# Attention with softmax split between ScalarE and VectorE: score units evacuated in pairs from two neighbouring PSUM banks

## The chip, the cores and the metric

The kernel runs on one core of a Trainium2 chip. The metric is device time in microseconds (us), the median of several executions. Engine names: TensorE (PE in the profile; PEld is its weight load), VectorE (DVE), ScalarE (ACT), GpSimd (POOL) and SyncE (SP), which issues DMA transfers. PSUM is the accumulator memory that TensorE writes: 8 banks, each holding 128x512 values of fp32 in this kernel.

## The reference

One transformer block with adaptive layer norm, for 2048 tokens of width 640, 32 heads of 20 columns, in bf16. The vector c gives six modulation rows (shift, scale and gate of each half).

```python
h = _layernorm(x) * (1 + ca) + sa
qkv = (h @ wqkv).reshape(B, S, 3, H, Dh)           # H = 32, Dh = 20
scores = einsum('bhqd,bhkd->bhqk', q, k) * Dh ** (-0.5)
o = einsum('bhqk,bhkd->bhqd', softmax(scores), v)
x = x + ga * (o @ wo)
h = _layernorm(x) * (1 + cb) + sb
x = x + gb * (((h @ w_gate) * (h @ w_up)) @ w_down)   # F = 1536
```

The scores are 32 x 2048 x 2048 numbers, and each goes through an exponential.

## The kernel before, in words

**Chunks, items, units.** The queries are cut into five chunks (`CHUNKS`: three of 512 and two of 256). A chunk has eight items; an item is four heads, one on each 32-row strip of TensorE. The scores of an item are made in units: one head's 128x512 block of transposed scores, which fills one PSUM bank (in a chunk of 256 queries a unit holds two key blocks). A score visit of TensorE (line 1403) writes several units; units on different row strips run side by side.

**Two ways to the exponential.** Most units go to ScalarE. Two or three of them form a group, which lies in neighbouring banks and is read by one ACTIVATE (line 1439, `fexp`) of 128x1024 or 128x1536 into the buffers PP. Even groups use set A of banks, odd ones set B; group g of `glist` is scored as soon as ScalarE has read the group before it in the same set. From group 580 (`HEADG`) on, even groups have three units.

The other units go to VectorE. They come in quads of four units, one per row strip; `QUADS` gives the number of quads of each item. A unit of a quad is scored as a passenger of a score visit (`d_attach`), into a bank of the shared pool G. VectorE evacuates it with one TENSOR_SCALAR of 128x512 (line 1463, `fp1`, called P1) into a quarter of a DB buffer as int16: add a bias, clamp at zero. This number's bits, read as bf16, approximate the exponential. When the quad is whole, two bit operations of 128x2048 (lines 1495 and 1503) and one multiplication (line 1500) make two correction terms in DSS, both of which TensorE multiplies with V (line 1957), beside the exponentials of ScalarE.

**What else uses PSUM.** Bank 7 collects the output of the current item. Pool G (banks 5, 6 and 2) also serves every round of the other stages: projections (lines 1062, 1126), V, output projection and feed-forward (lines 862 and 866), transposes and warm-up rounds. GX and GC serve the head of the program. Set A has banks 0, 1 (and 2 from group 580 on, when it leaves G), set B banks 3 and 4.

**What sets the order.** A planner written into the kernel (`Sched`) makes the order of every engine when the program is built: it steps through an assumed time with assumed durations, and emits fixed instruction streams with semaphore waits. `pick_pe` chooses TensorE's next work: a score visit if its banks are free, else value products, else rounds of other stages. `d_attach` adds up to two quad units to a visit, if in the planner's time a bank of G is free and the unit is due (`due`, from `D_LEAD`). Rounds of the other stages have a gate, a group number before which they may not start (`GATE_F`, `LATE_A`, `LATE_L`); `steal` gives ScalarE an evacuation when it would idle. The constants at the top steer these choices.

**The suffix.** After each chunk come its output projection, second layer norm and feed-forward. That of one chunk is spread between the visits of the next chunk; that of the last chunk stands behind the last exponential: output projection (line 862), residual sum (1682), statistics (1696), normalisation (1703), transposes (1715), evacuation with scale and shift into h2Tc (1731 and 1733), gate and up rounds (862), product hprodc (1784), down projection, residual sum (1838), store. The matmuls that remain of the fourth chunk's down projection (line 866, wd and hprodt) stand in between. With `T_SPLIT` the h2Tc evacuations of the last chunk are made per 128 tokens.

Of the kernel before, what the change touches and what calls it, by code (L numbers as in the profile page):

```python
# [12 lines left out]
SEM = 60.0  # L13
# [12 lines left out]
DMA_SLOW = 0.0015  # L26
DMA_LAT = 1700.0
STEAL_END = 66197.894
STEAL_GAP = 184.697
HAM_W = 3413.3  # L30
HAM_MIN = 2550.0

# [288 lines left out]
def emit_program(nc, sched, nsem_dma=56):  # L321
# [83 lines left out]
    with nc.Block() as block:  # L405
# [20 lines left out]
        def _(e):  # L426
# [4 lines left out]
CHUNKS = ((0, 512), (512, 512), (1024, 512), (1536, 256), (1792, 256))  # L431
QUADS = ((0, 4, 3, 3, 4, 3, 4, 3),
         (3, 4, 3, 4, 3, 3, 4, 4),
         (3, 3, 4, 4, 3, 4, 4, 4),
         (1, 2, 1, 2, 1, 1, 1, 2),
         (1, 1, 1, 1, 0, 1, 1, 1))
D_LEAD = 0.383
NB0, NSS = 2, 3
HEADG = 580
OP_EARLY = 1  # L440
EV_OP = 0.5
T_SPLIT = 1
GU_OUTER = 4
TAIL_PRE = 1
LN2T = 0.6
# [2 lines left out]
X_LAST = 2  # L448
X_TAIL = 0
XBACK = 1  # L450
HOLD = 110
PVTOL = 253
XDPRIO = 2.163
TPRIO = 0.75
TAHEAD = 1
GU_ONE = 1
# [3 lines left out]
NPS = 4  # L460
TS_4X, TT_2X = 600.0, 1145.0
WM_GATE = 9
WM_NEED = 1.814
K_DIRECT = (0, 1, 2, 3)
Q_DIRECT = 2
K_LEAD = 0.705
K_ALL = (0,)
KD_LEAD = 0.216
DMA_WINDOW = 900000
D_LATE = 16  # L470
D_RES = 58
PVMIN, PVMAX, PVCAP = 4, 14, 13
PV0 = 0
V_PARTS = [[0, 4], [4, 8]]
V_L1 = 0.2
# [7 lines left out]
PREEMPT = 0.0  # L483
PRE_M = 0.3
PV0N = 1
GATE_F = (0.925, 0.688, 1.105, 0.744, 1.0)
FILL_MIN = 4156.882
FILL_HARD = 0.0
FILL_T0, FILL_TH, FILL_MINH = 2300.0, 17000.0, 7500.0
FILL_MODE = 'P'  # L490
# [2 lines left out]
LN_POOL = ()  # L493
LN_ACT = [1, 3, 5, 7]
XFIRST = 0
LN2P = 2.447
NALT = 1
OPFIRST = 0
HT_L = 0.105
V_L = 0.225  # L500
LATE_A = 4.5
LATE_L = 2.493
LATEQ = (3,)
LATEQ_A = 2
LATEQ_F = 0.581
QUAD_GAIN = 0.597233983857778
NTERM = 2
XHALF = 1
X_LATE = -0.231
X_HALF = 0.0  # L510


# [8 lines left out]
def build_kernel(nc, A_x, A_wqkv, A_wo, B_x, B_w_gate, B_w_up, B_w_down, c, w_mod, out):  # L521
# [53 lines left out]
    def bank(b):  # L575
        return ps[:, b, :]
# [112 lines left out]
            stx.append(C.alloc("stx", [128, 2, KD, 128], BF16))  # L689
        nsq, nsx = nsx, len(stx)  # L690

    G = Slots([5, 6, 2] if HEADG else [5, 6], "G")
    GX = Slots([3, 4] if HEADG else [2, 3, 4], "GX")
    hx = (1, 3) if HEADG else (1, 3, 4)
    GC = Slots([0, 1], "GC")
    BPV = 7
# [577 lines left out]
    while ap < NA:  # L1274
        even = len(glist) % 2 == 0
        us = ubuf[ap:ap + (3 if even and len(glist) >= HEADG else 2)]
        apos.append(ap)
        ap += len(us)
        glist.append((us, 0 if even else 3))
    NG = len(glist)  # L1280
    sc.ng = NG
    gstart = []
# [109 lines left out]
    def unit_score_deps(u):  # L1392
        d = list(qt_ready[(u.j, u.ci)])
        for kt in u.kts:
            hv = kt_half.get((u.j, kt // 4))
            d += kt_ready[(u.j, kt // 4)] if hv is None else [hv[kt % 4 // 2]]
        d = list(dict.fromkeys(d))
        return d
# [58 lines left out]
    for qi, (it, us) in enumerate(dquads):  # L1457
        st_ = d_state[qi]
        for x, u in enumerate(us):
            cell = {}  # L1460

            def fp1(e, st_=st_, x=x, cell=cell):
                return e.tensor_scalar(DB0[:, st_["slot"], x * 512:(x + 1) * 512], bank(cell["b"]), EBIAS, 0.0,  # L1463
                                       op0=ALU.add, op1=ALU.max)
            tp = Task("dve", ps_cost(512), fp1, [], prio=0.8, name=f"P1.{qi}.{x}")
            tp.on_start = lambda task, cell=cell: G.done(cell["b"], task)
            u.task = (tp, cell)
            sc.left += 1
            st_["p1"][x] = tp
# [644 lines left out]
    def d_attach(ts, t, pos, rows, limit, relax):  # L2114
        n = 0
        while n < limit:
            if not dst["left"]:
                if dst["next"] >= len(dlist) or due[dst["next"]] > pos:
                    break
                dst["left"] = list(dlist[dst["next"]:dst["next"] + 4])  # L2120
                dst["fresh"] = True
            if due[dst["next"]] > pos:
                break
            pick = None
            for u in dst["left"]:
                if (u.s not in rows or relax) and all(d.done is not None and d.done + SEM <= t for d in unit_score_deps(u)):
                    pick = u
                    break
            if pick is None:
                break  # L2130
            ga = G.avail()
            if ga is None or ga[0] > t:
                break
            st_ = d_state[pick.quad[0]]
            if dst["fresh"]:
                ba = sB0.avail()
                if ba is None or ba[0] > t:
                    break
                st_["slot"], rel = sB0.take(ba[1], NTERM)
                st_["brel"] = rel  # L2140
                dst["fresh"] = False
            b, rel = G.take(ga[1], 1)
            tp, cell = pick.task
            cell["b"] = b
            ts.deps = ts.deps + unit_score_deps(pick) + rel
            ts.emits = ts.emits + unit_score_emits(pick, lambda b=b: bank(b))
            tp.deps = [ts] + st_["brel"]
            sc.left -= 1
            sc.add(tp)
            rows[pick.s] = rows.get(pick.s, 0) + 1  # L2150
            dst["left"].remove(pick)
            dst["next"] += 1
            n += 1
        return n

    def pick_pe(t):
# [44 lines left out]
        elif not tail_added[0]:  # L2201
            tail_added[0] = True
            la = [a for a in act_tasks[-2:]]
            if all(a.done is not None for a in la):
                for b in range(5):
                    if b != 2 or not HEADG or back[0]:
                        G.add(b, la)
            else:
                tail_added[0] = False
# [143 lines left out]
```

## Time and profile before

| | us |
|---|---|
| median of 3 executions | 817.66 |
| lowest, highest | 817.46, 822.7 |
| the profiled execution | 816.77 |
| its span, first to last instruction | 815.0 |
| first exponential of line 1439 starts | 16.3 |
| last exponential ends | 782.4 |
| transpose of the last item of each chunk (line 1587) | 218.6, 402.4, 585.1, 686.1, 783.1 |

Read from the profiled execution: "busy" is the time in which an engine had an instruction of the kind in work; "x" is how many; the number behind the comma is the mean length of one in ns; what stands behind the bar is idle time just ahead of it, and what ended it. Records of neighbouring instructions on one engine overlap, so the mean length is more than the time from one start to the next. A row of the stretches has the window, its length, the busy time, the count, the clock that TensorE was granted (1.00 is full), the share of DMA and GB/s; an instruction that crosses an edge counts in both windows. A row of the waits has who waited, for whom, the sum in us, how often, and the longest. A row of the timeline has start and length in us, with equal neighbours merged.

### The profile page before, as it was taken

How to read it: one execution, taken by the hardware profiler on the slowest of the kernel's cores; microseconds unless marked ns; L12 is line 12 of the kernel's file. 1: busy time of each engine (PE TensorE's matmuls, PEld its weight loads, DVE VectorE, ACT ScalarE, POOL GpSimd, SP SyncE). 2: the span in 40 equal slices, each digit the busy share in tenths (PEclk: the TensorE clock that was granted, in tenths of full speed). 3: DMA queues.
4: the chain of work that ended last, by engine and by line, in shares of the span. 5: the costliest groups of instructions: out<-in, count | busy, mean ns of one | idle time of the engine just before them, and what ended most of it. 6: DMA issues, size and time to landing. Idle time of an engine off the chain costs nothing.

```text
span 815.0 us, 29082 instructions
## 1 busy us (share of the span) xinstructions
PE 787.8 (97%) x12581; PEld 306.3 (38%) x12581; DVE 722.7 (89%) x1272; ACT 775.9 (95%) x821; POOL 73.3 (9%) x105
## 2 busy tenths in 40 slices
PE   9999999999999999999999999999989999999998
PEld 4433333322232332233333223333243344554557
DVE  7989999999989999999999999999998877676663
ACT  6889999999999999999999999999999999999952
POOL 3300000000011000000001000000021000000000
PEclk9999999999999999999999999999999999999999
DMA  9724311113500225100400222002100236116610
GB/s 294 222 84 103 77 39 38 49 49 116 126 19 25 51 66 160 39 5 28 95 6 12 49 53 55 6 20 61 47 8 14 55 86 130 44 31 137 133 37 17
DMA packets 116446, 54.73 MB, mean 67 GB/s; under 512 B 83915, under 2 KB 116319, under 8 KB 116319
## 3 DMA queue, kind: packets, MB, share of 16 engines
q1 hardware_dynamic: 115391, 51.72, 24.8%
q8 instruction: 100, 1.64, 0.9%
q10 hardware_dynamic: 928, 1.15, 0.4%
q14 instruction: 27, 0.22, 0.1%
HBM read 41.85 MB, written 8.41 MB: 62 GB/s over the span
## 4 chain that ended last, share of the span: by engine, by line
ACT 44%; PE 37%; issue 9%; DVE 9%; DMA 1%; ACTq 0%; DVEq 0%
ACT PP L1439 44%; PE ps_all L1403 11%; PE ps_all L866 10%; PE ps_all L1957 7%; DVE DB L1463 3%; PE ps_all L862 3%; PE ps_all L1126 3%; PE ps_all L1062 2%; DVE DSS L1500 1%; DMA wm<-in_w_mod_dram 1%; DVE DSS L1495 1%; DVE DSS L1503 1%; PE ps_all L1023 1%; PE ps_all L887 0%; DVE st L1696 0%
## 5 line engine op out<-in xcount | busy, mean ns | idle before, releaser
L1439 ACT ACTIVATE PP<-ps_all 128x1024 bf16<-128x1024 f32 (+1 forms) x777 | 756.9, 1202 | 5.4 <-PE ps_all L1403 3.9
L1403 PE MATMUL ps_all<-QT,KT 32*128 32x512 bf16 (+1 forms) x2560 | 309.0, 340 | 17.4 <-ACT PP L1439 13.5
L1463 DVE TENSOR_SCALAR DB<-ps_all 128x512 int16<-128x512 f32 x396 | 263.1, 682 | 35.4 <-PE ps_all L1403 34.2
L1403 PEld LDWEIGHTS ps_all<-QT,KT 32*128 32x128 bf16 x2560 | 81.5, 91 | 262.3 <-ACT PP L1439 232.4
L1957 PE MATMUL ps_all<-PP,Vf 128*32 128x512 bf16 (+2 forms) x2092 | 164.3, 342 | 0.1
L1500 DVE TENSOR_TENSOR DSS<-DB,DSS 128x2048 bf16<-128x2048 bf16 x99 | 122.0, 1232 | 0.0
L866 PE MATMUL ps_all<-h2T,stg 128*32 128x512 bf16 (+1 forms) x1808 | 116.7, 338 | 1.6 <-DVE DB L1463 1.1
L1592 POOL TENSOR_TENSOR OTn<-OT,invT 128x512 bf16<-128x512 f32 (+1 forms) x39 | 43.1, 1104 | 604.8 <-DVE invT L1590 604.8
L1957 PEld LDWEIGHTS ps_all<-PP,Vf 128*32 128x32 bf16 (+1 forms) x2092 | 47.2, 94 | 85.2 <-issue 78.5
L1957 PE MATMUL ps_all<-DSS,Vf 128*32 128x512 bf16 (+3 forms) x936 | 77.4, 350 | 0.2
L1495 DVE TENSOR_SCALAR DSS<-DB 128x2048 int16<-128x2048 int16 x99 | 68.2, 689 | 0.8
L1503 DVE TENSOR_SCALAR DSS<-DB 128x2048 int16<-128x2048 int16 x99 | 68.1, 688 | 0.9 <-PE ps_all L1957 0.9
L866 PE MATMUL ps_all<-wd,hprod 128*32 128x320 bf16 (+1 forms) x1364 | 57.9, 280 | 0.1
L866 PEld LDWEIGHTS ps_all<-h2T,stg 128*32 128x32 bf16 x1808 | 40.3, 95 | 36.9 <-issue 17.1
L866 PEld LDWEIGHTS ps_all<-wd,hprod 128*32 128x32 bf16 x1364 | 30.7, 96 | 18.4 <-issue 10.4
L866 PE MATMUL ps_all<-wV,hT 128*32 128x320 bf16 (+1 forms) x704 | 31.6, 289 | 0.1
L1957 PEld LDWEIGHTS ps_all<-DSS,Vf 128*32 128x32 bf16 (+1 forms) x936 | 23.4, 95 | 21.9 <-issue 9.1
L1126 PE MATMUL ps_all<-hT,wq 128*32 128x512 bf16 x375 | 31.1, 382 | 0.2
L1815 DVE TENSOR_TENSOR hprod<-ps_all,gsb 128x512 bf16<-128x512 f32 x36 | 24.6, 684 | 6.0 <-PE ps_all L866 6.0
L866 PE MATMUL ps_all<-wo,Ocp 128*32 128x320 bf16 (+1 forms) x620 | 28.8, 288 | 0.4 <-DVE DB L1463 0.2
L1587 DVE STREAM_TRANSPOSE OT<-ps_all 128x512 f32<-128x512 f32 (+1 forms) x40 | 24.2, 604 | 4.3 <-PE ps_all L1957 4.2
L2277 PE MATMUL ps_all<-ident 128*32 128x512 bf16 x308 | 27.3, 383 | 0.3 <-DVE DB L1463 0.2
(122 smaller groups left out, 516.8 us busy)
## 6 DMA issues: line engine op xcount, KB each, us to landing
stg<-in_B_w_gate_dram SPq DMA_DIRECT2D x50, 160.0 KB
stg<-in_B_w_up_dram SPq DMA_DIRECT2D x50, 160.0 KB
QT<-q_rows SPq DMA_DIRECT2D x22, 128.0 KB
KT<-k_rows SPq DMA_DIRECT2D x84, 32.0 KB
wm<-in_w_mod_dram SPq DMA_DIRECT2D x3, 800.0 KB
x<-in_A_x_dram SPq DMA_DIRECT2D x7, 320.0 KB
xck<-in_A_x_dram SPq DMA_DIRECT2D x3, 640.0 KB
wd<-in_B_w_down_dram SPq DMA_DIRECT2D x1, 1920.0 KB
```

What stands on the lines that cost most here:

```text
L866: return lambda e, b: e.matmul(ps[32 * x:32 * x + 32, b, c0 + o:c0 + o + w], lhs()[:, 32 * x:32 * x + 32], rhs() if w == n else rhs()[:, o ...
L1126: f = [lambda e, b_, k=k, x=x: e.matmul(ps[x:x + min(32, w - x), b_, :], wx[:, k, r0 + x:r0 + min(x + 32, w)], hT[tc][:, k, :], tile_posit ...
L1403: ems.append(lambda e, i=i, kt=kt: e.matmul(dstf()[:, i * u.n:(i + 1) * u.n], KT[32 * u.s:32 * u.s + 32, u.j, kt * 128:(kt + 1) * 128], QT ...
L1439: return e.activation(PPs[g % 2][:, cellp["p"], 0:nu * 512], ps[:, b0:b0 + nu, :].rearrange("p b c -> p (b c)"), AFT.Exp, scale=ESCALE)
L1463: return e.tensor_scalar(DB0[:, st_["slot"], x * 512:(x + 1) * 512], bank(cell["b"]), EBIAS, 0.0, op0=ALU.add, op1=ALU.max)
L1495: return e.tensor_scalar(DSS[:, st_["ss"][0], :], DB0[:, st_["slot"], :], 0x7F, 0x3F00, op0=ALU.bitwise_and, op1=ALU.bitwise_or)
L1500: return e.tensor_tensor(d, DB0[:, st_["slot"], :].bitcast(BF16), d, ALU.mult)
L1503: return e.tensor_scalar(DSS[:, st_["ss"][1], :], DB0[:, st_["slot"], :], 0x7F80, 2, op0=ALU.bitwise_and, op1=ALU.bitwise_or)
L1592: f3 = lambda e: e.tensor_tensor(OTn[:, 0:n].rearrange("p (b c) -> p b c", c=32), OT[:, 0:n].rearrange("p (b c) -> p b c", c=32), invT[:, ...
L1815: f = lambda e: e.tensor_tensor(hprod[:, fc, 0:n], ps[:, r.b["b"], 0:n], gsb[:, gs, 0:n], ALU.mult)
L1957: ems.append(lambda e, i=i, kt=kt, stt=stt, stp=stp: e.matmul(ps[32 * s:32 * s + mc, BPV, 0:u.n], Vf[:, (kt * H + 4 * u.j + s) * VW:(kt * ...
L2277: task.emits = [lambda e, x=x: e.matmul(ps[32 * x:32 * x + 32, b_, :].rearrange("p (a b) -> p a b", a=4), ident[:, 32 * x:32 * x + 32], id ...
```

## The change

When a unit of a quad is attached to a score visit, a second unit of the same quad is now looked for (its inputs there, its row strip not used in the visit, due as well). If in the planner's time two neighbouring shared banks are free, (3, 4) or else (2, 3), both are scored in that visit, into these banks, and one TENSOR_SCALAR of 128x1024 evacuates both; the output goes to two quarters of DB, which need not lie side by side. Otherwise a unit goes alone, as before. The planner counts 1120 ns for a pair.

So that the shared banks are neighbours, the bank map changes: G is now banks 4, 3 and 2, and set B (the odd groups) and GX are banks 5 and 6. Some thirty constants of the planner differ, among them the quads per item (chunk 2 has one fewer, the last chunk two more), the leads and gates, the limit of value products per turn (`PVCAP`), and `T_SPLIT`, which is off.

```diff
-STEAL_GAP = 184.697
+STEAL_GAP = 115.475
...
-         (3, 3, 4, 4, 3, 4, 4, 4),
+         (3, 3, 4, 4, 3, 4, 4, 3),
          (1, 2, 1, 2, 1, 1, 1, 2),
-         (1, 1, 1, 1, 0, 1, 1, 1))
-D_LEAD = 0.383
+         (2, 1, 1, 1, 0, 2, 1, 1))
+D_LEAD = 0.34
...
-T_SPLIT = 1
+T_SPLIT = 0
...
-K_LEAD = 0.705
+K_LEAD = 0.693
...
-D_RES = 58
-PVMIN, PVMAX, PVCAP = 4, 14, 13
+D_RES = 114
+PVMIN, PVMAX, PVCAP = 4, 14, 10
...
-GATE_F = (0.925, 0.688, 1.105, 0.744, 1.0)
+P1_PAIR = 1
+P1_PCOST = 1120.0
+GATE_F = (0.91, 0.621, 0.409, 0.425, 1.0)
...
-LATE_A = 4.5
-LATE_L = 2.493
+LATE_A = 3.033
+LATE_L = 3.352
...
-    G = Slots([5, 6, 2] if HEADG else [5, 6], "G")
-    GX = Slots([3, 4] if HEADG else [2, 3, 4], "GX")
+    G = Slots([4, 3, 2], "G")
+    GX = Slots([5, 6], "GX")
...
-        glist.append((us, 0 if even else 3))
+        glist.append((us, 0 if even else 5))
...
             def fp1(e, st_=st_, x=x, cell=cell):
+                if len(cell["bs"]) == 2:
+                    (ba, bb), (xa, xb) = cell["bs"], cell["xs"]
+                    return e.tensor_scalar(
+                        DB0[:, st_["slot"], :].rearrange("p (x c) -> p x c", c=512)[:, xa:xb + 1:xb - xa, :],
+                        ps[:, ba:bb + 1:bb - ba, :], EBIAS, 0.0, op0=ALU.add, op1=ALU.max)
...
-            b, rel = G.take(ga[1], 1)
+            mate = None
+            if P1_PAIR and limit - n >= 2:
+                for u in dst["left"]:
+                    if u is not pick and (u.s not in rows or relax) and all(
+                            d.done is not None and d.done + SEM <= t for d in unit_score_deps(u)):
+                        mate = u
+                        break
+                av = [i_ for i_, r_ in G.free if all(z.done + SEM <= t for z in r_)]
+                two_ = next(((i_, i_ + 1) for i_ in (3, 2) if i_ in av and i_ + 1 in av), None)
+                if two_ is None:
+                    mate = None
+                if mate is not None and due[dst["next"] + 1] > pos:
+                    mate = None
...
+            b, rel = G.take(ga[1] if mate is None else G.avail(two_[0])[1], 1)
...
+            if mate is not None:
+                b2, rel2 = G.take(G.avail(two_[1])[1], 1)
+                two = sorted((pick, mate), key=lambda u: u.quad[1])
+                lo_, hi_ = min(b, b2), max(b, b2)
+                ts.deps = ts.deps + unit_score_deps(mate) + rel2
...
+                cell["bs"] = [lo_, hi_]
+                cell["xs"] = [u.quad[1] for u in two]
...
+                tp.dur = P1_PCOST
```

## The prediction, made before the result was known

> **What bounds the kernel now.** I read the busy shares first, then ScalarE's busy time stretch by stretch, then the waits, and last the timeline of the end. The first part of the page has
>
> ```profile
> span 815.0 us, 29082 instructions
> PE 787.8 (97%) x12581; PEld 306.3 (38%) x12581; DVE 722.7 (89%) x1272; ACT 775.9 (95%) x821; POOL 73.3 (9%) x105
> ```
>
> Three engines look full, so shares do not decide. The busy time of the exponentials alone (line 1439), by stretches, does:
>
> ```profile
> 16.00:110.00 94.00, 84.91 (x92) 1.00 0.44 123
> 110.00:160.00 50.00, 49.70 (x55) 1.00 0.14 37
> 160.00:260.00 100.00, 99.97 (x110) 1.00 0.27 71
> 260.00:360.00 100.00, 100.00 (x111) 1.00 0.25 65
> 360.00:460.00 100.00, 100.00 (x111) 1.00 0.14 34
> 460.00:560.00 100.00, 100.00 (x110) 1.00 0.14 34
> 660.00:783.00 123.00, 122.43 (x109) 1.00 0.40 88
> ```
>
> From 160 us to the last exponential (it ends at 782.4 us) ScalarE does nothing else and never rests. One 128x1024 exponential goes by every 0.905 us: some 110.5 in 100 us, the edges counted once. Its mean record is 1156 ns, because the records of two neighbours overlap. The waits say the same from the other side:
>
> ```profile
> PEld ps_all L1403 <- ACT PP L1439: 232.4, 641, 1.2
> PEld ps_all L866 <- DVE DB L1463: 13.1, 40, 0.8
> PEld ps_all L1403 <- DVE DB L1463: 5.3, 14, 0.6
> ```
>
> TensorE, about to score, waits for ScalarE to free a bank, 0.36 us each time (232.4 / 641); it waits for a VectorE evacuation of line 1463 rarely. So the time is a head of 16.3 us to the first exponential, 766 us at ScalarE's pace, and a tail of 32.6 us after the last one. A VectorE instruction counts only if it holds ScalarE up, or takes units from it.
>
> **The change, part by part.** I counted the instructions of the built programs, old and new.
>
> *The pair.* 25 evacuations of 128x1024 appear, and 350 of 128x512 stay (before: 396). So only 50 of 400 units are paired: 2, 9, 12, 2 and 0 pairs in the five chunks. The price on VectorE comes from these rows:
>
> ```profile
> L1463 DVE TENSOR_SCALAR DB<-ps_all 128x512 int16<-128x512 f32 x396 | 263.1, 682 | 35.4 <-PE ps_all L1403 34.2
> L1777 DVE CAST gsb<-ps_all 128x256 bf16<-128x256 f32 x12 | 5.0, 415 | 1.5 <-PE ps_all L866 1.5
> 301.27 1.88 DVE L1463 TENSOR_SCALAR DB<-ps_all 128x512 int16<-128x512 f32 x3
> ```
>
> 256 more elements cost 682 - 415 = 267 ns, so 512 more cost 534 ns, and I estimate 1216 ns for the record of a pair. Three in a row take 1.88 us, so each further one 0.60 us; a pair then occupies 0.60 + 0.53 = 1.13 us where two singles occupy 1.20. The saving is 0.07 us back to back, and 2 x 682 - 1216 = 148 ns if the two stood apart: 1.7 to 3.7 us of VectorE over 25 pairs. No 128x1024 read by VectorE stands in the trace; a read that crosses banks into two strips could also cost more, up to two full records (1364 ns), which is 4 us lost. All of it lies on an engine that doesn't set the end, so its direct worth on the path is nothing; if that cover went, it would cost those 4 us at most.
>
> [...] The rows give a fixed part of 0.07 us per instruction (0.60 less 0.53). [...]
>
> *The quads.* Chunk 2 has one quad fewer and the last chunk two more (99 to 100 in all). ScalarE loses four units, and the count shows how: 677 exponentials of 128x1024 instead of 679, still 98 of 128x1536. That is 2 x 0.905 = **1.8 us off the bound engine**. In exchange VectorE does one more quad: four evacuations at 0.60, two of 0.69 and one of 1.23, together 5.0 us, less the pairs' 1.7 to 3.7. But it moves from where VectorE is full to where it isn't: it is busy 194.3 of 200 us from 360 to 560, and 83.9 of 123 from 660 on. So chunk 2 is relieved by one quad (5.0) and 12 pairs (0.8 to 1.8), and the last chunk takes 10 us into some 39 us of idle time. I cost that at nothing; the cover is this idle time, and if it weren't there ScalarE would have to wait for up to 10 us.
>
> *The bank map and the constants.* Banks change their owners, not their number: three shared ones before, three after. ScalarE's order is the same in both programs up to the last exponential, early evacuations that it takes over included, and TensorE's first 385 instructions are the same, so the head stays: nothing. Score visits that name a VectorE semaphore are 303 in both. The other constants shift where feed-forward and projection work stands between visits; its amount is equal, with 6 fewer warm-up rounds. The cost lies between what ScalarE still loses and what a late visit costs, taken up below; I put it at nothing, since the exponentials of 660 to 783 us still ran at 122.43 of 123 beside a TensorE as full as it will be.
>
> *The tail.* This is the one place where work moves onto the path. Down-projection rounds of the fourth chunk (output of line 866, from wd and hprodt) come to 192 full matmuls. Before, 44 of them stood ahead of the last exponential's end and 148 behind; now all 192 stand behind. The timeline of TensorE:
>
> ```profile
> 786.04 3.99 PE L866 MATMUL ps_all<-wd,hprodt 128*32 128x320 bf16 x112
> ...
> 791.24 0.48 PE L1715 MATMUL ps_all<-ident,xn2c 128*128 128x128 bf16 x5
> 791.65 0.59 PE L866 MATMUL ps_all<-wd,hprodt 128*32 128x320 bf16 x12
> ```
>
> 28 rounds of four in 3.99 us, the first 0.32: 0.136 us a round, so the 44 extra cost 1.5 us of TensorE. Part of it fills gaps, as TensorE waited there for the layer norm. In the new order 144 matmuls follow 786.04, to 790.95; then 8 transposes (0.5), 4 matmuls and 2 transposes with their switches (0.5), 40 matmuls (1.45): the gate and up rounds start at 793.4, where they started at 792.50. Eight more second-term matmuls before the last transpose of the output add 0.1. T_SPLIT = 0 makes five wide evacuations of ten narrow ones; the 40 matmuls (1.45 us) hide them, and without that cover the last would cost one more 0.41. So **+1.0 us**, between 0 (all 44 in gaps) and 2.0 (none, and an evacuation bare).
>
> Sum: -1.8 + 1.0 = -0.8 us. The profiled execution took 816.77 us (span 815.0 and 1.8 around it), which gives 816.0. The median of the runs shown is 817.66, 0.9 above that execution, and gives 816.9. I forecast the middle, **816.4 us**. A measurement of this kernel can tell about 1% (8 us) from no change, and this is a tenth of it.
>
> **The rivals.**
>
> *Slower: the pair keeps two of three shared banks.* A pair lets its first bank go 0.53 us later than a single would, and TensorE takes its work in a fixed order: a feed-forward round that needs the bank waits, and the next score visit stands behind it. Place: chunks 1 and 2 (about 219 to 585 us by the transposes of line 1587), with 21 of the pairs, where VectorE has 3% idle time. For it: the 40 waits of line 866 on line 1463, up to 0.8 us. Against it: 0.36 us of slack ahead of each visit, and a pair is only formed when both banks are free. If 0.53 - 0.36 = 0.17 us passes through at each, 25 x 0.17 = 4.3 us on top of the forecast, and the time is 820.7. With no slack it is 25 x 0.53 = 13 us, 829.7. It decides for slower by over 1% from about 9 us, which is 0.36 us lost per pair, slack gone at two thirds of them. Chance 0.09 for that, 0.12 for the mild case.
>
> *Faster: late stalls go.* ScalarE without an exponential lost 9.1 us between 16 and 110 us, of which some 2.5 us is its other work there (three evacuations of Vf, one of QT, one of KT), and under 1 us in the stretches after 110 us up to 560. If relief of VectorE gave back 4 of it, the time would be 812.4. Against it: the early orders are the same in both programs, and the early chunk has two pairs. Chance 0.08. Beyond 1% all 6 us of these stalls would have to go and the tail cost nothing: 1.8 + 6.6 = 8.4 us, 808.4 by the profiled execution: 0.05.
>
> *It doesn't do what it says.* Partly so already: only an eighth of the units pair. If pairs gave nothing and the added quad cost ScalarE waits worth its 1.8 us, what is left is the tail's +1.0, 818.2. It belongs to the forecast's own chance.
>
> **How the numbers follow.** Forecast with its own bounds (within 2 us) 0.66, mild loss 0.12, mild gain 0.08, loss over 1% 0.09, gain over 1% 0.05. Within 1% is 0.66 + 0.12 + 0.08 = 0.86. The range runs from the mild gain to the mild loss with the tail's upper bound, 812 to 822, and leaves out the two outer cases.
>
> **What would show it.** The pair's record near 1.22 us; 775 exponentials, still some 110 in 100 us from 160 on, the last one ending near 780.6 us; from there to the end 33.6 us instead of 32.6; VectorE busier after 660 us. I am wrong if exponentials fall under 109 in 100 us in a stretch between 160 and 560 us, if TensorE's waits on the pairs (line 1467 of the changed kernel) reach 10 us, or if the last exponential ends where it did.

## The result and the profile after

| | before | after |
|---|---|---|
| median, us | 817.56 (6 runs, 816.67 to 822.7) | **826.84** (6 runs, 825.72 to 829.87) |
| profiled execution, us | 816.77 | 825.72 |
| span | 815.0 | 823.9 |
| exponential instructions | 777 | 775 |
| first one starts, last one ends | 16.3, 782.4 | 16.4, 789.75 |
| from there to the end of the span | 32.6 | 34.2 |

The changed kernel is slower: ratio 1.011, interval 1.0092 to 1.0128. Of the 8.9 us between the spans, 7.3 are lost before the last exponential ends and 1.6 behind it. First a row of the page of before, its exponentials:

```profile
L1439 ACT ACTIVATE PP<-ps_all 128x1024 bf16<-128x1024 f32 (+1 forms) x777 | 756.9, 1202 | 5.4 <-PE ps_all L1403 3.9
```

Then the page of the changed kernel: span, busy time by engine, and the rows of the exponential (line 1441), of the single evacuation (1470) and of the pair (1467).

```profile
span 823.9 us, 28833 instructions
...
PE 790.0 (96%) x12485; PEld 307.1 (37%) x12485; DVE 727.3 (88%) x1252; ACT 773.9 (94%) x816; POOL 70.4 (9%) x105
...
L1441 ACT ACTIVATE PP<-ps_all 128x1024 bf16<-128x1024 f32 (+1 forms) x775 | 755.9, 1218 | 14.0 <-PE ps_all L1405 9.3
...
L1470 DVE TENSOR_SCALAR DB<-ps_all 128x512 int16<-128x512 f32 x350 | 234.7, 683 | 43.9 <-PE ps_all L1405 43.1
...
L1467 DVE TENSOR_SCALAR DB<-ps_all 128x1024 int16<-128x1024 f32 x25 | 30.4, 1214 | 0.2 <-PE ps_all L1405 0.2
```

The pair does what it says, and its record is as long as was forecast. The end of the row of line 1441 is the finding: ScalarE is idle ahead of exponentials for 14.0 us, where it was 5.4. The stretches of this line tell where:

```profile
16.00:110.00 94.00, 81.25 (x87) 0.98 0.43 119
110.00:160.00 50.00, 48.63 (x54) 1.00 0.14 41
160.00:260.00 100.00, 99.38 (x109) 1.00 0.27 69
260.00:360.00 100.00, 99.74 (x110) 1.00 0.26 69
360.00:460.00 100.00, 100.00 (x110) 1.00 0.12 30
460.00:560.00 100.00, 100.00 (x110) 1.00 0.15 35
560.00:660.00 100.00, 98.83 (x89) 0.98 0.16 38
660.00:783.00 123.00, 121.52 (x108) 1.00 0.42 90
```

From 260 to 560 us, where 20 of the 25 pairs stand, 0.3 us is lost. The loss is in the first and in the last stretches, and the granted clock (fifth column), 1.00 throughout before, is below it in two. The waits of TensorE's weight loads speak against the rival of the held banks:

```profile
PEld ps_all L1405 <- ACT PP L1441: 240.9, 659, 1.2
...
PEld ps_all L868 <- DVE DB L1470: 6.1, 19, 1.1
...
PEld ps_all L868 <- DVE DB L1467: 0.7, 3, 0.3
```

Rounds of line 868 (866 before) waited 13.1 us for evacuations before, and 6.1 + 0.7 now. Pairs are hardly waited for, 1.2 us in all.

The exponentials of both kernels can be compared one by one, since ScalarE's order is the same up to the last one. Start of the exponential with a given index, after less before:

| index | 60 | 80 | 130 | 140 | 600 | 610 | 700 | 710 | 774 |
|---|---|---|---|---|---|---|---|---|---|
| us | +0.86 | +4.41 | +4.53 | +5.93 | +6.05 | +7.76 | +7.27 | +8.56 | +9.22 |

So it is lost in steps: 3.5 us near 90 us, 1.4 near 155, 1.7 near 595, 1.3 near 708, and small ones. The two exponentials fewer give 1.9 back (9.22 to 7.3 at the last one's end).

**Step at 89 us.** The timeline of the changed kernel:

```profile
88.00 2.22 SPq L1619 DMA_DIRECT2D Ocp<-OcT  x3
...
88.88 0.66 PE L868 MATMUL ps_all<-wmb,SCb 128*32 128x320 bf16 x16
...
90.33 0.87 SPq L1196 DMA_DIRECT2D QT<-q_rows  x2
91.25 1.54 SPq L1619 DMA_DIRECT2D Ocp<-OcT  x2
92.38 0.13 PEld L1405 LDWEIGHTS ps_all<-QT,KT 32*128 32x128 bf16 x3 [3.11 <-issue]
...
92.85 1.02 ACT L1441 ACTIVATE PP<-ps_all 128x1024 bf16<-128x1024 f32 x1 [2.50 <-PE ps_all L1405]
92.85 0.69 DVE L1470 TENSOR_SCALAR DB<-ps_all 128x512 int16<-128x512 f32 x1 [2.67 <-PE ps_all L1405]
```

All engines stand still together, which no bank or buffer explains, and the wait is put down to "issue". The visit at 92.41 carries a VectorE unit of the fourth item as a passenger. In the built program it waits for the load of that item's Q, which SyncE issues at 90.33, behind a queue of other transfers. Before:

```profile
89.53 0.90 SPq L1194 DMA_DIRECT2D QT<-q_rows  x2
...
93.98 0.40 PE L1403 MATMUL ps_all<-QT,KT 32*128 32x512 bf16 x4
```

The same load was issued at 89.53, and the first visit that needs it, that of group 75, ran at 93.98, so nobody waited; in the changed kernel the visit of group 70 is the first. The planner's time has the load of the changed kernel issued at 85.89 us, 4.4 us before SyncE did it, and landed 0.4 us ahead of the visit. And the clock falls behind the gap (PE busy in each window, instructions, clock):

```profile
88.00:92.00 4.00, 1.54 (x37) 1.00 0.28 80
92.00:96.00 4.00, 3.59 (x36) 0.67 0.64 137
96.00:100.00 4.00, 4.00 (x65) 0.90 0.01 4
```

**Steps at 155 and 708 us.** ScalarE waits for value products of line 1965, which free the buffers PP; TensorE has rounds of other stages in front of them. ScalarE's timeline:

```profile
158.62 1.94 ACT L1441 ACTIVATE PP<-ps_all 128x1024 bf16<-128x1024 f32 x2 [1.18 <-PE ps_all L1965]
161.01 1.02 ACT L1441 ACTIVATE PP<-ps_all 128x1024 bf16<-128x1024 f32 x1 [0.45 <-PE ps_all L1965]
...
708.19 1.45 ACT L1441 ACTIVATE PP<-ps_all 128x1536 bf16<-128x1536 f32 x1 [1.17 <-PE ps_all L1965]
```

**Step at 592 us.** TensorE has little to do at 588 to 592, no gap over 0.94 us though, and then the clock falls (0.61 is the mean of the row; the last section has the fall itself):

```profile
588.00:592.00 4.00, 2.52 (x43) 0.96 0.13 45
592.00:596.00 4.00, 4.00 (x52) 0.61 0.58 164
```

### The profile page after: what moved, and what is told of

The parts are those of the page before. It is cut to its first block, busy times and chain, and to the rows that moved or that the text cites. A ratio compares the mean times of both kernels' runs of the same rounds, so it can differ in the third digit from the quotient of the medians.

```text
span 823.9 us, 28833 instructions
## 1 busy us (share of the span) xinstructions
PE 790.0 (96%) x12485; PEld 307.1 (37%) x12485; DVE 727.3 (88%) x1252; ACT 773.9 (94%) x816; POOL 70.4 (9%) x105
## 4 chain that ended last, share of the span: by engine, by line
ACT 46%; PE 37%; issue 10%; DVE 5%; DMA 1%; ACTq 0%; DVEq 0%
ACT PP L1441 46%; PE ps_all L868 12%; PE ps_all L1405 11%; PE ps_all L1965 8%; PE ps_all L864 3%; DVE DB L1470 1%; PE ps_all L1128 1%; PE ps_all L1064 1%; DMA wm<-in_w_mod_dram 1%; DVE DSS L1511 1%; PE ps_all L1025 1%; DVE DSS L1503 1%; DVE DSS L1508 1%; DVE DB L1467 0%; PE ps_all L2326 0%
## 5 line engine op out<-in xcount | busy, mean ns | idle before, releaser
L1470 DVE TENSOR_SCALAR DB<-ps_all 128x512 int16<-128x512 f32 x350 | 234.7, 683 | 43.9 <-PE ps_all L1405 43.1
L1600 POOL TENSOR_TENSOR OTn<-OT,invT 128x512 bf16<-128x512 f32 (+1 forms) x39 | 41.2, 1056 | 648.3 <-DVE invT L1598 641.6
L1965 PE MATMUL ps_all<-DSS,Vf 128*32 128x512 bf16 (+1 forms) x960 | 79.2, 351 | 1.5 <-DVE DSS L1511 1.4
L1503 DVE TENSOR_SCALAR DSS<-DB 128x2048 int16<-128x2048 int16 x100 | 68.9, 689 | 1.2
L1511 DVE TENSOR_SCALAR DSS<-DB 128x2048 int16<-128x2048 int16 x100 | 69.7, 697 | 0.0
L868 PE MATMUL ps_all<-wd,hprod 128*32 128x320 bf16 (+1 forms) x1320 | 60.3, 284 | 0.0
L868 PEld LDWEIGHTS ps_all<-wd,hprod 128*32 128x32 bf16 x1320 | 30.6, 96 | 19.3 <-issue 10.9
L1965 PEld LDWEIGHTS ps_all<-DSS,Vf 128*32 128x32 bf16 x960 | 24.3, 95 | 24.0 <-issue 9.7
L1467 DVE TENSOR_SCALAR DB<-ps_all 128x1024 int16<-128x1024 f32 x25 | 30.4, 1214 | 0.2 <-PE ps_all L1405 0.2
```

The costliest lines, as they stand in the source:

```text
L868: return lambda e, b: e.matmul(ps[32 * x:32 * x + 32, b, c0 + o:c0 + o + w], lhs()[:, 32 * x:32 * x + 32], rhs() if w == n else rhs()[:, o ...
L1467: return e.tensor_scalar(DB0[:, st_["slot"], :].rearrange("p (x c) -> p x c", c=512)[:, xa:xb + 1:xb - xa, :], ps[:, ba:bb + 1:bb - ba, :] ...
L1503: return e.tensor_scalar(DSS[:, st_["ss"][0], :], DB0[:, st_["slot"], :], 0x7F, 0x3F00, op0=ALU.bitwise_and, op1=ALU.bitwise_or)
L1511: return e.tensor_scalar(DSS[:, st_["ss"][1], :], DB0[:, st_["slot"], :], 0x7F80, 2, op0=ALU.bitwise_and, op1=ALU.bitwise_or)
L1600: f3 = lambda e: e.tensor_tensor(OTn[:, 0:n].rearrange("p (b c) -> p b c", c=32), OT[:, 0:n].rearrange("p (b c) -> p b c", c=32), invT[:, ...
L1965: ems.append(lambda e, i=i, kt=kt, stt=stt, stp=stp: e.matmul(ps[32 * s:32 * s + mc, BPV, 0:u.n], Vf[:, (kt * H + 4 * u.j + s) * VW:(kt * ...
```

## The experiments

**Theory A**: the loss comes from the order that the planner laid with the new constants, place by place (a late load, value products behind rounds, stretches in which TensorE has little work). **Theory B**: the pairs cost it by holding two banks. A third suspect is the bank map. The "index" below is that of the table above.

| run | median, us | ratio to before, 95% |
|---|---|---|
| bank map alone (e2b_map_only) | 818.43 | 0.9997 to 1.0016 |
| pairs split (f1_split_pairs) | 825.58 | 1.0073 to 1.0111 |
| no late load (f2_other_q) | 823.09 | 1.0051 to 1.0087 |
| visits doubled (f3_double) | 826.47 | 1.0092 to 1.0122 |
| no late load, some visits doubled (f9_keep_busy) | 820.32 | 1.0026 to 1.0055 |
| five causes at once (f7_all) | 822.87 | 1.0043 to 1.0084 |
| 44 matmuls out of the tail (f8_tail44) | 826.11 | 1.0076 to 1.0134 |
| T_SPLIT on (e4_tsplit) | 827.27 | 1.0103 to 1.0134 |
| constants without pairs (e1_no_pair) | 824.68 | 1.0071 to 1.0105 |
| pairs without constants (e2_pair_in_before) | 833.65 | 1.0172 to 1.0210 |
| before, one constant nudged (g1_nudge) | 824.19 | 1.0060 to 1.0120 |
| order searched, 18 pairs (h1_pairs18) | 820.00 | 1.0012 to 1.0045 |
| order searched, 10 pairs (h2_pairs10) | 817.99 | 0.9992 to 1.0011 |
| order searched, 18 pairs (h3_pairs18b) | 817.59 | 0.9992 to 1.0011 |

### The bank map alone

```diff
-P1_PAIR = 1
+P1_PAIR = 0
-STEAL_GAP = 115.475
+STEAL_GAP = 184.697
... (every other constant as before)
```

> The kernel before with its own constants, and only the bank map of the changed kernel (shared banks 4, 3 and 2, odd groups in 5 and 6); no pairs; every engine has the order of the kernel before. If the map by itself costs nothing, 816.7 to 818.5 us and exponentials within 0.3 us of before throughout. If neighbouring banks disturb each other (VectorE reading bank 4 beside TensorE writing 5), exponentials or evacuations get longer and the time rises by 2 us or more.

Measured: 818.43 us, not to be told from 817.59 beside it. The map costs nothing that can be measured. The second half of the expectation, exponentials within 0.3 us of before throughout, held up to index 223 only: the profiled execution (819.01) lost 1.0 us there and 1.1 us at index 756, each behind a late load (0.82 us for Ocp, 1.14 us for stg).

```profile
232.43 0.32 PE L868 MATMUL ps_all<-wo,Ocp 128*32 128x320 bf16 x4 [0.82 <-DMA Ocp<-OcT]
```

This is the order of before, so that order too has loads on the edge, which come late in some executions.

### The pairs split, in the same order

```diff
                 tp.dur = P1_PCOST
+                tp.emits = [lambda e, c_=cell, i_=i_: e.tensor_scalar(
+                    DB0[:, c_["st"]["slot"], c_["xs"][i_] * 512:(c_["xs"][i_] + 1) * 512],
+                    bank(c_["bs"][i_]), EBIAS, 0.0, op0=ALU.add, op1=ALU.max) for i_ in range(2)]
```

> The changed kernel, every engine in the same order, but each of the 25 pairs is evacuated by two instructions of 128x512 instead of one of 128x1024; TensorE still scores both units in one visit. Theory A (the 9 us come from where the new constants put loads and rounds of other stages, at five places, and not from the pairs): 826 to 828 us, the last exponential within 0.6 us of the changed kernel's 789.75. Theory B (the wide instruction holds two shared banks too long, and the visits behind it are late): the first bank comes free 0.5 us earlier at each pair, and the time falls by 4 to 9 us, to 817 to 822. A loss of 2 us or more would say that the pair instruction is a gain by itself.

Measured: 825.58 us, 1.3 under the changed kernel's median, with overlapping intervals; so at most a small part of the 9 us. It is 0.4 under theory A's range and far from theory B's. The profiled execution is no help with the 1.3: its last exponential ended later, at 791.2 (the expectation had it within 0.6 us of 789.75), because the clock stayed low longer after the 89 us gap (0.54 and 0.60 in 92 to 100 us) and the step there was 5.2 instead of 3.5 us. The steps at 89, 155 and 708 us stand at the same places; that at 592 us is missing, and one of 1.2 us stands at 615 us, where the clock fell instead (0.90 and 0.68 in 608 to 616 us). Theory B is refuted as the cause of the loss; whether the wide instruction costs something up to 1.3 us stays open.

### No late load

```diff
+    def qj(u):
+        return 2 if u.is_d and u.item == 3 else u.j
...
-        d = list(qt_ready[(u.j, u.ci)])
+        d = list(qt_ready[(qj(u), u.ci)])
...
-                QT[u.ci][32 * u.s:32 * u.s + 32, u.j, :], tile_position=(32 * u.s, 0)))
+                QT[u.ci][32 * u.s:32 * u.s + 32, qj(u), :], tile_position=(32 * u.s, 0)))
```

> The changed kernel, every engine in the same order, but the VectorE units of the fourth item are scored with the Q of the third item, which lies in SBUF already; so the score visit at 89 us has no load to wait for. (The scores of those units are then another item's: that part of the computation is changed, its amount is not.) Theory A: the gap of 3.1 us on TensorE at 89.3 us goes, the granted clock stays at 1.00 between 92 and 100 us (it was 0.67 and 0.90), and the time falls by 2.9 us for the wait and up to 1.5 us for the slow clock after it: 821.5 to 823.5 us. If the late load is only the first of several things that are late there, the exponential of index 90 gains under 1 us on the changed kernel's and the time stays at 825 to 827. Theory B says nothing of this place and expects no change.

Measured: 823.09 us, 3.75 less than the changed kernel. The same windows of this kernel:

```profile
88.00:92.00 4.00, 4.00 (x74) 1.00 0.26 69
92.00:96.00 4.00, 4.00 (x63) 1.00 0.66 143
96.00:100.00 4.00, 4.00 (x53) 1.00 0.14 46
```

Theory A had 821.5 to 823.5. At index 80 the lag on before is -0.02 us instead of +4.41, so gap and slow clock together are 4.4 us, and nothing else is late there. The last exponential ends at 785.36, 4.4 earlier. Not all of it showed in the profiled execution, because the tail had a stall of its own: the first output projection of the last item waited for its loads, and the clock fell to 0.71 after it.

```profile
786.66 1.29 PE L864 MATMUL ps_all<-wo,Ocp 128*128 128x320 bf16 x5 [1.99 <-DMA Ocp<-OcT]
```

The order of the changed kernel has this load on the edge as well; in its own profile it came in time, in the kernel with T_SPLIT on it was 1.87 us late.

### Keeping TensorE busy around 590 us

```diff
+    for ts, us in score_q[596:612]:
+        ts.emits = ts.emits + ts.emits
```

> The changed kernel, every engine in the same order, but the score visits of groups 596 to 611 (about 580 to 594 us) write each of their matmuls twice, which keeps TensorE busier there. Theory A, last part (the granted clock fell to 0.61 at 592 to 596 us because TensorE had little work before): the clock stays at 1.00 in 588 to 596 us, the jump of 1.6 us between the exponentials 600 and 610 goes, and the time falls to 824.5 to 825.5 us. Its rival: the clock falls for a reason that has nothing to do with how busy TensorE is; then the jump stays, and the doubled matmuls at the low clock add some tenths: 826.5 to 828.

Measured: 826.47 us, no gain. But the profile separates two things:

```profile
588.00:592.00 4.00, 3.69 (x68) 1.00 0.11 36
592.00:596.00 4.00, 3.74 (x76) 1.00 0.54 159
...
608.00:612.00 4.00, 2.58 (x52) 0.95 0.03 7
612.00:616.00 4.00, 4.00 (x72) 0.62 0.04 8
```

With more work the clock holds at 592, and falls instead behind the next thin stretch, at 612. And the doubled visits cost time themselves where an exponential waits for them: 0.9 us between index 590 and 600. So only visits were doubled next whose exponentials come later than they must, on top of the kernel without the late load:

```diff
+    for ts, us in score_q[601:605] + score_q[614:620]:
+        ts.emits = ts.emits + ts.emits
```

> The changed kernel, every engine in the same order, without the late load (the fourth item's VectorE units use the third item's Q), and with only those score visits written twice that run where ScalarE still has groups in hand: 601 to 604 and 614 to 619. There TensorE was busy 2.5 of 4 us, and the clock fell behind it. If the fall is due to little work on TensorE, and the doubled visits of the earlier kernels ate the gain, the clock stays at 1.00 from 580 to 630 us and the time is 1.0 to 2.0 us under the kernel without the late load (823.1): 821.1 to 822.1. If the clock falls at another place all the same, or the doubled visits cost as much, 822.5 to 824.5.

Measured: 820.32 us, 2.8 under the kernel without the late load and better than expected (1.65 from fastest to fastest run; the profile shown for the other held the stall in the tail). The windows:

```profile
584.00:588.00 4.00, 3.13 (x66) 1.00 0.13 45
588.00:592.00 4.00, 3.60 (x72) 1.00 0.59 164
...
604.00:608.00 4.00, 3.19 (x85) 1.00 0.05 12
608.00:612.00 4.00, 4.00 (x106) 1.00 0.03 7
```

The clock stays full over the whole execution, and the last exponential comes another 1.0 us earlier. So more work on TensorE made the kernel faster, and the fall of the clock behind thin stretches is shown as a cause. It is worth 1.0 us by the last exponential and 1.65 by the fastest runs; the kernel without the late load had its fall at 606 us (0.75 and 0.82 in 604 to 612 us), not at 592.

### Five causes at once, and the tail

Groups 596 to 611 and 617 to 623 doubled, the late load gone, and these rounds thinned:

```diff
+    LESS = ("V13.1", "Kp3.3", "V14.1", "V15.1", "Qp3.0", "K6.0", "g2.10", "u2.10", "g2.11", "u2.11")
+    for nm in LESS:
+        r = sorted((t for t in sc.all if t.eng == "pe" and t.name == nm), key=lambda t: t.start)
+        for t in r[1:-1]:
+            if not t.deps:
+                t.emits = []
+    r = sorted((t for t in sc.all if t.eng == "pe" and t.name == "dn3.0"), key=lambda t: t.start)
+    for t in r[1:11] + r[13:14]:
+        t.emits = []
```

> The changed kernel, every engine in the same order, pairs as they are, with the five suspected causes taken away at once: the fourth item's VectorE units use the third item's Q (no late load at 89 us); score visits of groups 596 to 611 and 617 to 623 write their matmuls twice (no idle TensorE ahead of 592 and 612 us); the inner steps of six projection rounds at 149 to 160 us and of four gate and up rounds at 698 to 707 us are left out, and 44 matmuls of the fourth chunk's down projection behind the last exponential. Theory A: 4.4 us, 1.6, 1.5, 1.3 and 1.5 come back, together 10.3 from 826.8: 815.5 to 818.5 us. Theory B: the loss is spread over the pairs, and the time stays above 821 us.

Measured: 822.87 us, 4.4 above theory A's range and, by the number alone, where theory B had it; the steps tell the two apart, as they stand at few places and not at the pairs. The late load was gone as before. The doubled visits cost 3.0 us between index 590 and 630. The thinned rounds at 155 us gave back 0.6: the step there went from 1.4 to 0.8, since the value products still stand behind rounds in a fixed order. With the rounds at 698 to 707 us thinned, the clock, 1.00 there in the changed kernel, fell to 0.57 in 700 to 704 us, behind 3.24 us of work in 4, and the step there grew to 1.6. So the amount of work on TensorE was not what those two steps consist of; their cause, the place of the value products in the order, is argued from the waits and not shown by a run. The last part of the edit, alone (last three lines of the diff):

> The changed kernel, every engine in the same order, without 44 of the 192 matmuls of the fourth chunk's down projection that stand behind the last exponential (that part of the output is not whole). If they make the longer tail, the time from the last exponential's end to the end of the span falls from 34.15 us to 32.6 to 33.0, and the time by 1.2 to 1.6 us, to 825.2 to 825.7. If they lie in the gaps that the layer norm leaves on TensorE, the tail stays within 0.5 us, and TensorE shows a wait for the layer norm instead (line 1711 or the h2Tc evacuations).

Measured: 826.11 us, and from the last exponential's end to the end 33.6 instead of 34.2: about 0.5 of the 1.5 us that these matmuls take. The second expectation came true:

```profile
797.89 0.62 PE L1723 MATMUL ps_all<-ident,xn2c 128*128 128x128 bf16 x8 [0.93 <-DVE xn2c L1711]
```

TensorE now waits 0.93 us for the layer norm, behind which two thirds of the extra matmuls had been hidden. T_SPLIT on:

> The changed kernel with T_SPLIT on again: only the order behind the last exponential differs. If the tail's loss (34.15 us instead of 32.57) comes from the five wide evacuations of h2Tc, it goes: 34.15 falls to 32.6 to 33.1, and the time to 824.5 to 825.7. If it comes from the 44 matmuls of the fourth chunk's down projection that now stand behind the last exponential, which this kernel leaves where they are, the tail stays within 0.4 us of 34.15, and the time at 826 to 827.

Measured: 827.27 us, no gain; its profiled tail (36.2) holds the 1.87 us wait for the load of Ocp told above, and 34.3 is left without it. So T_SPLIT is probably not the tail's loss; the late load keeps the run from showing it.

### Constants without pairs, pairs without constants, and neither

```diff
-P1_PAIR = 1
+P1_PAIR = 0
```

> The changed kernel with its bank map and all its constants, but pairs are never formed (P1_PAIR = 0): 400 single evacuations, and the planner orders anew from the first place where a pair stood, at about 57 us. Its first VectorE unit of the fourth item stands one score visit later than in the changed kernel. Theory A (loss by places, caused by the order): the wait at 89 us shrinks from 3 us to between 0 and 2 us with what follows it, other places fall as the new order has them: 820 to 826 us. Theory B (pairs cost by holding banks): the whole loss goes, 817 to 819 us. If the constants alone carry the loss and pairs nothing, 826 to 828 us.

Measured: 824.68 us, inside theory A's range. The lag on before at index 80 is +0.1 us: the wait is gone, as the load is issued at 86.88 us, 3.5 us earlier, and the visit of group 72 is the first that needs it. But at 154 us there is a step of 2.5, where ScalarE waits 2.09 us for value products, and others follow (1.2 between index 490 and 520, 2.1 near 635), and the tail is 35.8 us. The clock was 1.00 throughout this execution, so a new order can lose all this without a fall of the clock.

```profile
154.39 2.86 ACT L1441 ACTIVATE PP<-ps_all 128x1024 bf16<-128x1024 f32 x3 [2.09 <-PE ps_all L1965]
```

The other way round (new code, but all constants and quads of before; 36 pairs, not the 27 that the expectation counts):

> The kernel before with its own constants and quads, plus the new bank map and pairs (27 of them). In its order a score visit takes a VectorE unit of the fourth item about as early as the changed kernel does, ahead of that item's Q load. Theory A: one jump of 3 to 5 us between the exponentials 60 and 80, at 88 to 100 us, and under 0.5 us at any other place of the stretch from 160 to 585 us, where most pairs stand: 820 to 823 us. Theory B: the lag grows by 0.2 to 0.5 us with each pair through the second and third chunks, without a jump at 89 us: 822 to 830 us. If pairs are harmless wherever they stand and the load is in time, 816 to 818 us.

Measured: 833.65 us, slower than either theory had it. Theory A's jump at 89 us isn't there (-0.1 at index 70); theory B's steady growth isn't either: from index 160 to 580, past some 25 pairs, the lag goes from 2.7 to 3.4. There is a step of 2.9 at 150 us, 5.6 us between index 590 and 650, where the clock fell to 0.50 to 0.73 twice, and a tail of 41.1 us, because the fourth chunk's feed-forward was pushed back:

```profile
794.81 3.13 PE L868 MATMUL ps_all<-h2Tt,stg 128*32 128x256 bf16 x108
...
801.01 2.37 PE L868 MATMUL ps_all<-h2Tt,stg 128*32 128x256 bf16 x80
...
804.37 6.70 PE L868 MATMUL ps_all<-wd,hprodt 128*32 128x320 bf16 x192
```

All of that stands behind the last exponential. The constants without pairs lose 7 us, the pairs without constants 16, both together 9: they don't add up, so neither is "the" cost. The decisive question is then: what does any new order cost? The kernel before, old map, no pairs:

```diff
-D_LEAD = 0.383
+D_LEAD = 0.375
```

> The kernel before, with its bank map, no pairs, and one constant nudged by 2%: D_LEAD 0.375 instead of 0.383, which moves VectorE units by some visits and lets the planner order the rest anew. If what costs time is only that the order was laid anew (theory A, carried further: the constants of the kernel before fit its own order, and another order loses at the crowded places), it is 3 to 8 us slower, 820.5 to 826, with single jumps of 0.5 to 2.5 us at the places between 130 and 150, 590 and 640, 690 and 720 (counted in exponentials). If a new order is as good as the old one by itself, and pairs or the large moves of the constants cost the time, 816.7 to 818.7 us.

Measured: 824.19 us, 6.8 slower, ratio 1.0060 to 1.0120. One constant moved by 2% costs nearly as much as the change. Its steps: 1.8 us near index 225, 3.5 near 629 (ScalarE waits 3.12 us for value products), 2.0 near 695, where the clock fell to 0.66, and 1.0 near 766 (of the three places expected, the first was wrong). The first and the last are waits for loads:

```profile
232.93 0.32 PE L866 MATMUL ps_all<-wo,Ocp 128*32 128x320 bf16 x4 [1.76 <-DMA Ocp<-OcT]
```

The kernel with the map alone lost 1.0 and 1.1 us to the same two loads in the order of before, so up to 2 us of the profiled 8 may be the execution and not the new order. The fastest of the six runs, 822.96, is still 6 us over the fastest of before.

### Pairs in an order that was looked for

The planner returns the time at which its own last task ends. It is an assumption built into the kernel and no measurement, but it can be set beside the measured times (all plan ends are given 2.4 us under the value returned):

| kernel | plan ends, us | measured | measured less plan |
|---|---|---|---|
| before | 806.3 | 817.6 | 11.3 |
| changed kernel | 808.9 | 826.8 | **18.0** |
| constants without pairs | 813.8 | 824.7 | 10.9 |
| pairs without constants | 822.5 | 833.7 | 11.1 |
| one constant nudged | 811.4 | 824.2 | 12.8 |
| h1_pairs18 | 808.6 | 820.0 | 11.4 |
| h2_pairs10 | 807.4 | 818.0 | 10.6 |
| h3_pairs18b | 807.0 | 817.6 | 10.6 |

So most of these orders cost about what their plan says, and the changed kernel alone has some 7 us that its planner did not foresee (the nudged one 1.7). The last three kernels came from a search over constants and over the visits at which a pair is allowed, for an early end of the plan with loads well ahead of their use (here the third):

```diff
+PAIR_AT = (251, 397, 419, 547, 571, 627, 701, 709, 713, 745, 899, 921, 925, 941, 1063, 1105, 1230, 1240)
...
-            if P1_PAIR and limit - n >= 2:
+            if pos in PAIR_AT and limit - n >= 2:
...
-D_LEAD = 0.383
+D_LEAD = 0.433
-GATE_F = (0.925, 0.688, 1.105, 0.744, 1.0)
+GATE_F = (0.995, 0.867, 0.827, 1.072, 1.0)
...
```

> Pairs with an order looked for anew: from the kernel before, pairs allowed at 18 named places only, one quad more in the first chunk, and some fifteen constants moved so that the planner's own end comes as early as a search found and loads stand earlier ahead of their use. In the planner's own time it ends at 808.6 us, where the kernel before ends at 806.3, the changed kernel at 808.9, the pairs without the constants at 822.5 and the constants without pairs at 813.8; on the chip those came out 11.3, 18.0, 11.1 and 10.9 us after that. Theory A (an order costs what its plan says, and pairs cost nothing beyond it, unless a load comes late or the clock falls): 808.6 + 11.1 = 819.7, within 1.5 us, and no jump at 89 us. Theory B (each pair costs 0.2 to 0.5 us by holding banks): 4 to 9 us more, 823 to 829 us.

> The same with another order from that search: 10 pairs, the quads of the kernel before, and the planner's own end at 807.4 us. Theory A: 807.4 + 11.1 = 818.5, within 1.5 us. Theory B: 2 to 5 us more, 820.5 to 824 us. A time under 816.7 would make it faster than the kernel before; neither theory expects that.

> Pairs at 18 named places in a third order of the search; the quads of the kernel before; the planner's own end at 807.0 us. Theory A (plan plus 11.1): 818.1, within 1.5 us; the other order with 18 pairs, planned at 808.6, took 820.0. Theory B (each pair costs 0.2 to 0.5 us): as slow as that one or slower, 820 to 826 us.

Measured: 820.0, 817.99 and 817.59 us; theory A had 819.7, 818.5 and 818.1. The two kernels with 18 pairs lie 2.4 us apart, one of them level with the kernel before. The page of the third:

```profile
span 815.9 us, 28877 instructions
...
PE 786.5 (96%) x12505; PEld 306.4 (38%) x12505; DVE 722.3 (89%) x1252; ACT 774.7 (95%) x818; POOL 76.0 (9%) x105
```

And its row of the pair among the groups:

```profile
L1464 DVE TENSOR_SCALAR DB<-ps_all 128x1024 int16<-128x1024 f32 x18 | 21.9, 1216 | 1.8 <-PE ps_all L1402 1.7
```

So a kernel with 18 pairs can be level with the kernel before. What the pairs themselves cost or gain in that order isn't shown, as no run has the same order without them; as VectorE isn't what ends the span, no gain was to be expected. No order was found that beats the kernel before.

## Why the prediction was wrong

I forecast 816.4 us, range 812 to 822; it was 826.8.

- **The pair**: right. Estimated 1216 ns, measured 1214; 25 of them, and no run shows a gain from them.
- **The quads**: right in size. Two exponentials fewer are 1.8 to 1.9 us, and the table by index shows them. The waits of up to 10 us that VectorE's added quads in the last chunk might have caused didn't come: behind index 710 the lag grows by 0.7 us.
- **"The bank map and the constants ... I put it at nothing"**: this is the step that failed. The map is nothing, as a run shows; the order that the constants laid around the pairs is some 9 us, and 7 without the pairs. Two arguments carried the step. The first was "TensorE's first 385 instructions are the same, so the head stays: nothing". That is true of the 16.3 us to the first exponential (16.4 now), but the instructions that are the same end at 28 us. Exponentials start late from 49 us on, and 4.4 us were lost at 89 to 100 us: a unit moved ahead of its own Q load (3 us), and the slow clock after that. I had compared orders on ScalarE and counted waits on VectorE, but had not set each moved score visit against the DMA that it needs; the rows of before, 89.53 for the load and 93.98 for the first visit, leave 4.4 us, of which the load itself takes 2 (90.33 to 92.38 in the changed kernel), and I never looked at them. The second was that 660 to 783 us was full before and still in time. That showed that the order of before was in time, not that another would be: the nudged kernel has the same amounts of everything and is 6.8 us slower. The planner's own ends were not set beside each other either: 808.9 for the changed kernel and 806.3 for before, 2.6 us later, where the forecast had -0.8.
- **What took its place**, for the 8.9 us between the profiled spans: 3.5 near 89 us (4.4 shown by the run without the load, as the kernel before itself loses 0.8 there), 1.4 and 1.3 in front of late value products (argued), 1.7 behind a thin stretch of TensorE (1.0 to 1.7 shown, for a fall at a neighbouring place), 1.2 in small steps (not looked into), 1.6 in the tail, less 1.9 for the exponentials.
- **The tail, "+1.0 us, between 0 and 2.0"**: measured 1.6, inside. The gate and up rounds start 11.4 us after the last exponential's end, where it was 10.1. The run without the 44 matmuls puts 0.5 of that to them, less than I thought. The last block of output projections starts 0.78 us after the last exponential, where it was 0.38, and the transposes of the first tokens no longer stand ahead of the second half of the layer norm, as the wait of 0.93 us above shows; I had only the second-term matmuls for this, put at 0.1. The remaining 0.3 lies behind the last residual sum, in the store, and its cause is open.
- **The rivals**: slower by more than 1% came true, but not by the mechanism named. Waits on pairs are about 1 us, not 10, and the stretches from 260 to 560 us lost 0.3. "Fewer stalls" fell: idle time ahead of exponentials went from 5.4 to 14.0 us. Of the signs I had named, the last exponential told: it was to end near 780.6 and ended at 789.75. The other two stayed silent, as 109 to 110 exponentials still went by in each 100 us from 160 to 560, and the waits on pairs were 1.2 us: both look for a loss at the pairs, and it stood elsewhere.

## What to carry to other kernels

When constants of a planner move, its whole order moves, and the old order was the one that fitted: price a new order at several us (the nudge cost 6.8 here) until each moved instruction has been set against the transfers and buffers that it needs, and compare with a neutral nudge before blaming the edit. Look for gaps in which all engines stand still: here it was a load, and it was paid twice, once as a wait (3.11 us) and once as a slow clock after it (0.67 and 0.90 in 92 to 100 us), together 4.4 us. A widened instruction on an engine that doesn't end the span had no gain to show here (826.84 us with the pairs, 825.58 with each split in two).

## What the runs showed of the hardware

The clock fell without a long gap. Behind 2.52 us of work in 4, with no gap over 0.94 us (after, 588 to 592 us), it was 0.61 for the next 4 us; behind the gap at 89 us (3.11 us in the changed kernel) it was 0.54 to 0.74 in five executions. These are means of rows. In narrower windows each of the changed kernel's two falls ahead of the end of its span is 3.41 us at 0.50, one from 93.35 us on, the other from 591.70 us on:

```profile
588.29:591.70 3.41, 1.93 (x35) 1.00 0.15 53
591.70:595.11 3.41, 3.41 (x42) 0.50 0.68 191
```

The share of busy time does not decide it: 2.54 us of work in 4 was followed by full clock (after, 608 to 612 us, then 1.00), 3.24 by 0.57 (five causes at once, 696 to 700 us). What tells the two stretches apart was not shown.

The falls differ from execution to execution. By an estimate one fall lowers an execution's mean clock by 0.002 (half of 3.41 us in 824): the changed kernel's six have 0.998 (825.95 us) to 0.992 (829.87 us, the slowest), though the fastest, 825.72 us, has 0.996.

More work can be faster: with ten score visits written twice (820.32 us, 823.09 without) the last exponential came 1.0 us earlier, and the clock held (1.00 throughout).
